# An equivariant message-passing kernel with 24 indirect gathers and 176 TensorE products placed ahead of its first pass

## The chip, the cores and the metric

The kernel runs on one core of one Trainium2 chip. The metric is the device time of one execution, in microseconds. Before the change it is 10608.61 us, the median of 3 runs (10598.79 to 10617.41). The profile is of another execution of the same program; it shows each instruction of five engines: PE (TensorE, the matrix products), DVE (VectorE), ACT (ScalarE), POOL (GpSimd) and SP (SyncE, which mostly issues transfers). PEld is the weight load of TensorE.

## The reference

There are N = 10000 nodes with 64 channels of 4 components each (256 floats, 1 KB a node), and E = 640000 edges, each with a source node, a target node, 4 numbers Y and 4 features.

```python
def reference(x, src, dst, Y, edge_feat, w_rad, cg, w_mix):
    N, C, M = x.shape[0], x.shape[1], x.shape[2]          # 10000, 64, 4
    R = _silu(edge_feat @ w_rad)                          # (E, C)
    xs = x[src]                                           # (E, C, M): the gather
    tp = jnp.einsum('eci,ef,ifo->eco', xs, Y, cg)         # (E, C, M)
    msg = R[:, :, None] * tp
    agg = _segment_sum(msg.reshape(-1, C * M), dst, N).reshape(N, C, M)
    return jnp.einsum('ncm,cd->ndm', agg, w_mix)
```

## The kernel before, in words

The edges are sorted by target node on the chip, so that the sum over the edges of a node becomes products on TensorE. This takes three stages.

Pass 1 (`pass1`, with `tables` and `route`) deals the edges, in three parts, into 18 groups of target nodes. Chunks of 12 tiles of 128 edges are put in order by products with one-hot matrices (`move`, L602) and scattered into a buffer in device memory by an indirect transfer that POOL issues (`store`, L613, the tile `rt` into `grp`). Pass 2 does the same within each group, with buckets of 32 nodes (into `bkt`). The messages (`messages`) go bucket by bucket: `gather` (L893) issues one indirect transfer for each tile of 128 edges, which fetches 128 rows of `x` of 1 KB each into `xg`; DVE multiplies by the radial weights (L945); `sums` (L958) adds up on TensorE; `mix` (L1006) applies the last weights in 256-column products, and the result is written out. A third stage (`overflow`) treats edges that found no room, in a loop with a run-time count, at the very end.

The first part of pass 1 runs alone, and `groups` then runs all the rest interleaved: messages of one group, pass 2 of the next and pass 1 of the next part. The order within an engine is fixed in the program; each engine runs its own queue in order and waits on semaphores. Transfers that POOL issues go through one software queue with eight semaphores in turn, those of SP and ACT through hardware queues.

At the start, `run` (L1206) opens the pool `p1`, POOL clears the tile `z` (L1214), the constants are made on POOL and DVE (`consts`, L144), SP loads the first target and source numbers (`ends`, L672 and L673), and ACT's queue issues 18 transfers that clear the group buffers from `z` (L230). The first products on TensorE are the counts of L365. All on-chip memory is taken from pools; a tile whose memory was used before waits for what last used it.

The lines with numbers are those of the program before; in the changed program the lines up to L86 keep theirs, the others move by 2, and those of `run` and what follows by 57.

Of the kernel before, what the change touches and what calls it, by code (L numbers as in the profile page):

```python
# [18 lines left out]
F = mybir.dt.float32  # L19
BF = mybir.dt.bfloat16  # L20
I32 = mybir.dt.int32
OP = mybir.AluOpType
# [3 lines left out]
P = 128  # L26
# [19 lines left out]
class Pass:  # L46


    def __init__(self, T, r, cap, act, carry):
        self.T, self.r, self.cap, self.act, self.carry = T, r, cap, act, carry  # L50
        self.stride = 1 << (cap + P - 1).bit_length()
        self.rw = r * W

        assert T * P + B * (2 * r - 2 if carry else r - 1) < (P + 1) * r and cap >= P


def weave(main, side, ratio):

    acc = 0.0
    for said in main:  # L60
        acc += ratio
        while acc >= 1.0:
            acc -= 1.0
            next(side, None)
        yield said
    yield from side


def run(gen):
    for _ in gen:  # L70
        pass


class Kernel:
    def __init__(self, ctx, tc, x, src, dst, Y, ef, w_rad, cg, w_mix, out):
        self.ctx, self.tc, self.nc = ctx, tc, tc.nc
        self.N, self.E = x.shape[0], src.shape[0]
        assert self.E % P == 0
        self.NT = self.E // P
        self.x = x.rearrange("n c i -> n (c i)")  # L80
        self.src = src.rearrange("(p t) -> p t", p=P)
        self.dst = dst.rearrange("(p t) -> p t", p=P)
        self.Y = Y.rearrange("(p t) f -> p t f", p=P)
        self.ef = ef.rearrange("(p t) f -> p t f", p=P)
        self.w_rad, self.cg, self.w_mix = w_rad, cg, w_mix
        self.out = out.rearrange("n c o -> n (c o)")  # L86
        pool = lambda n, b, **k: ctx.enter_context(tc.tile_pool(name=n, bufs=b, **k))
        self.cst = pool("cst", 1)
        self.ps = pool("ps", 1, space=bass.MemoryType.PSUM)
        self.dr = pool("dr", 1, space=bass.MemoryType.DRAM)  # L90

        N, E, T, r = self.N, self.E, 12, 14
        assert N <= 1 << 14 and BT == sum(sum(u) for _, u in SPLIT)
        self.NG = (N + GN - 1) // GN
        assert self.NG <= B
        self.part, cut = [], 0
        for i, (share, _) in enumerate(SPLIT):
            end = cut + round(self.NT * share / (2 * T)) * 2 * T if i + 1 < len(SPLIT) else self.NT
            self.part.append((cut, end))
            cut = end  # L100
        self.gt = []
        for a, z in self.part:
            nch = (z - a + T - 1) // T
            e = [min(GN, N - g * GN) * (z - a) * P / N for g in range(self.NG)]
            self.gt.append([math.ceil((m + (r - 1) / 2 * nch + 3 * math.sqrt(m + (r * r - 1) / 12 * nch)) / P)
                            for m in e])
        NG = self.NG
        self.p1 = Pass(T, r, max(map(max, self.gt)) * P // r, 6, False)
        self.p2 = Pass(11, 15, BT * P // 15, 6, True)

        self.gbase = [[(k * NG + g) * self.p1.stride + self.p1.cap - self.gt[k][g] * P // r for g in range(NG)]
                      for k in range(len(SPLIT))]
        self.NBK = (N + NB - 1) // NB

        self.btile = [0]
        for _, u in SPLIT:
            self.btile.append(self.btile[-1] + sum(u))

        self.p1.ovf = len(SPLIT) * NG * self.p1.stride
        self.p2.ovf = self.NBK * self.p2.stride  # L120
        for q, tiles in ((self.p1, [z - a for a, z in self.part]), (self.p2, sum(self.gt, []))):
            q.none = -(-(q.ovf + sum((t + q.T - 1) // q.T for t in tiles) * P + 16) // q.stride) * q.stride
            q.rows = q.none
        self.p1.key, self.p2.key = "grp", "bkt"
        self.xw = max(q.T * q.rw for q in (self.p1, self.p2))
        assert max(q.T + q.carry for q in (self.p1, self.p2)) <= 12

        self.p1.NC, self.p2.NC = 24, max(-(-t // self.p2.T) for t in sum(self.gt, []))
        self.p1.dst = self.dr.tile([self.p1.rows, self.p1.rw], F, name="grp")
        self.p2.dst = self.dr.tile([self.p2.rows, self.p2.rw], F, name="bkt")  # L130

        self.sums = self.dr.tile([self.NBK, P, 256], F, name="sums")
        self.in_group = {"grp": 0, "bkt": 0}
        self.tab = {}
        self.held, self.wanted, self.pos = None, False, None
# [903 lines left out]
    def groups(self):  # L1039
# [26 lines left out]
        for v in range(4 * u):  # L1066
# [24 lines left out]
            next(main)  # L1091
        assert not later
        run(main)
        run(sort)

    def chunks(self, part):
# [21 lines left out]
    def overflow(self, ps, count):  # L1118
# [84 lines left out]
        with tc.For_i(0, n, 1) as k:  # L1203
            body(k)

    def run(self):  # L1206
        tile_pool, nc = self.tc.tile_pool, self.nc
        order = [self.NG - 1] + list(range(self.NG - 1))
        self.segs = [(k, g) for k in range(len(SPLIT)) for g in order]
        with tile_pool(name="p1", bufs=2) as self.ph:  # L1210
            self.rt_bufs, self.ls = 38, 8
            self.lag, self.ahead, self.early = 2, 3, 1
            self.z = self.ph.tile([P, 2048], F, name="z", bufs=1)
            nc.gpsimd.memset(self.z, 0.0)  # L1214
            self.consts()

            with self.tc.manual_schedule(engines={mybir.EngineType.SP}):
                first = self.pass1(0, 8)
                next(first)
                run(self.clear_groups(0, nc.scalar))  # L1220
                for _ in range(40):
                    next(first, None)
                while self.held:
                    next(first)
                self.weights()
                later = itertools.chain(self.clear_buckets(),
                                        *(self.clear_groups(k, nc.sync) for k in range(1, len(SPLIT))))
                run(weave(first, later, 0.185))
                self.sorted = 1
        with tile_pool(name="p2", bufs=2) as self.ph:  # L1230
            self.rt_bufs, self.ls = 5, 4
            self.lag, self.ahead, self.early = 1, 2, 0
            self.p1.NC = 14
            with self.tc.manual_schedule(engines={mybir.EngineType.PE, mybir.EngineType.DVE,
                                                  mybir.EngineType.Activation}):
                self.groups()
        with tile_pool(name="p3", bufs=1) as self.ph:
            self.overflow_consts()
            self.overflow(self.p1, self.kov[:, 0:1])
            self.overflow(self.p2, self.kov[:, 1:2])  # L1240
# [29 lines left out]
```

## Time and profile before

| | |
|---|---|
| median of the runs | 10608.61 us (10598.79 to 10617.41) |
| profiled execution: first to last instruction | 8660.7 us |
| profiled execution: a time of its own beside the span | none is given |
| PE busy | 6942.9 us |
| DVE busy | 7173.7 us |
| POOL busy | 6041.3 us |
| ACT busy | 4089.0 us |
| mean granted clock of TensorE | 0.894 |
| bytes moved by transfers | 1056.64 MB |

The span is 1947.9 us shorter than the median of the runs. Busy times are of each engine for itself; they overlap. Rows of the timeline give the start from the beginning of the span, the duration, the engine, the line, the operation, the tiles written and read, the shape and how many instructions are merged in the row, and in brackets the idle time of the engine just before with what ended it. A 32-bit floating-point product stands in the rows as two MATMUL records with a LDWEIGHTS each, a bfloat16 product as one.

### The profile page before, as it was taken

What the parts mean: (1) busy time and instruction counts of PE and PEld (TensorE: products, weight loads), DVE (VectorE), ACT (ScalarE), POOL (GpSimd) and SP (SyncE); (2) the same over time, 40 slices, a digit from 0 to 9 for tenths busy, and PEclk for the clock granted to TensorE, in tenths of its full rate; (3) what the DMA queues carried; (4) which work ended last, traced back from release to release, by engine and by line L of the source; (5) the groups of instructions that cost most, each with busy time, mean ns of one, the idle gap of its engine ahead of it and who ended that gap; (6) DMA issues with size and microseconds to landing.
All of it is one profiled execution on the core that took longest, in us unless ns stands there. A gap on an engine that the chain in (4) does not pass through costs nothing. (4 is left out here: it accounts for less than half of the span.)

```text
span 8660.7 us, 149335 instructions
## 1 busy us (share of the span) xinstructions
PE 6942.9 (80%) x52148; PEld 6380.0 (74%) x52148; DVE 7173.7 (83%) x13741; ACT 4089.0 (47%) x11736; POOL 6041.3 (70%) x6308
## 2 busy tenths in 40 slices
PE   7978888888888778888888888866888878788875
PEld 6867777777777677777777777766777767777764
DVE  8989899889998788999989998877877768677754
ACT  6866555555556455454544554433333323333310
POOL 1236777667777767777777777777777777777775
PEclk9989999889999889999889899888998889888887
DMA  9313434334433434444444444444444444444442
GB/s 169 104 58 99 123 115 119 103 113 117 121 110 111 122 106 132 135 132 138 133 130 136 135 133 134 128 138 132 128 125 125 125 124 124 122 128 125 124 123 83
DMA packets 696289, 1056.64 MB, mean 122 GB/s; under 512 B 252018, under 2 KB 500226, under 8 KB 695536
## 3 DMA queue, kind: packets, MB, share of 16 engines
q0 software_dynamic: 286560, 746.71, 30.3%
q1 hardware_dynamic: 406384, 292.76, 12.2%
q8 instruction: 412, 6.75, 0.3%
q10 hardware_dynamic: 2592, 7.63, 0.3%
q14 instruction: 341, 2.79, 0.1%
HBM read 856.08 MB, written 207.12 MB: 123 GB/s over the span
## 5 line engine op out<-in xcount | busy, mean ns | idle before, releaser
L893 POOL DMA_INDIRECT xg<-in_x_dram,sidx x5321 | 5067.8, 952 | 1739.3 <-issue 1386.5
L602 PE MATMUL pr<-X,oh 128*128 128x126 f32 (+1 forms) x21112 | 2765.2, 289 | 395.7 <-ACT rt L609 215.6
L958 PE MATMUL G<-S,xg 128*128 128x128 f32 x21284 | 2953.1, 302 | 98.1 <-DVE Gp L987 62.8
L602 PEld LDWEIGHTS pr<-X,oh 128*128 128x128 f32 x21112 | 2638.2, 201 | 477.8 <-ACT rt L609 264.2
L958 PEld LDWEIGHTS G<-S,xg 128*128 128x128 f32 x21284 | 2803.5, 215 | 139.3 <-DVE Gp L987 86.2
L945 DVE TENSOR_TENSOR xg<-xg,pre 128x1536 f32<-128x1536 f32 (+1 forms) x939 | 1556.8, 1658 | 710.5 <-DMA xg<-in_x_dram,sidx 586.4
L594 ACT ACTIVATE sq<-i,rowf 128x128 f32<-128x128 f32 x5605 | 1735.7, 393 | 13.9 <-DVE rowf L559 13.4
L572 DVE TENSOR_TENSOR X<-dv,Wt 128x1512 f32<-128x1512 f32 (+4 forms) x958 | 1588.4, 1658 | 149.0 <-PE pr L602 94.8
L927 ACT ACTIVATE pre<-pre 128x384 f32<-128x384 f32 (+1 forms) x939 | 430.8, 459 | 1694.7 <-PE pre L924 1204.7
L595 ACT ACTIVATE oh<-sq,ones 128x768 f32<-128x768 f32 (+3 forms) x958 | 932.1, 973 | 32.9 <-issue 5.5
L938 DVE TENSOR_TENSOR S<-dv,pay 128x768 f32<-128x768 f32 (+1 forms) x939 | 857.4, 913 | 48.0 <-PE G L958 2.8
L613 POOL DMA_INDIRECT grp<-rt,idx x417 | 415.5, 996 | 585.9 <-ACT rt L609 240.1
L588 DVE TENSOR_TENSOR oh<-dv,rowf 128x640 f32<-128x640 f32 (+2 forms) x922 | 792.2, 864 | 0.5
L613 POOL DMA_INDIRECT bkt<-rt,idx x541 | 543.2, 1004 | 221.7 <-issue 125.8
L911 PE MATMUL pre<-identb,e 128*108 128x128 bf16 x1878 | 277.3, 231 | 523.4 <-DVE xg L945 513.6
L911 PEld LDWEIGHTS <-e 128*108 128x108 bf16 x1878 | 219.9, 133 | 604.5 <-issue 515.2
L916 ACT ACTIVATE sT<-pre 108x256 bf16<-108x256 f32 x939 | 353.5, 376 | 631.1 <-PE pre L911 628.4
L1006 PE MATMUL po<-wf,Gs 128*128 128x256 f32 (+2 forms) x1392 | 382.3, 436 | 150.7 <-DVE Gs L987 150.5
L542 ACT ACTIVATE pc<-pp 128x432 f32<-128x432 f32 (+3 forms) x506 | 243.7, 482 | 524.1 <-DVE pos L551 407.3
L1006 PEld LDWEIGHTS po<-wf,Gs 128*128 128x128 f32 (+2 forms) x1392 | 277.5, 205 | 238.3 <-DVE Gs L987 166.8
L609 ACT ACTIVATE rt<-pr 128x135 f32<-128x135 f32 (+1 forms) x958 | 258.8, 273 | 269.4 <-DMA bkt<-rt,idx 181.4
L923 PE MATMUL pre<-wr,sT 108*128 108x192 bf16 x939 | 240.2, 256 | 142.2 <-ACT sT L916 141.8
(240 smaller groups left out, 5309.3 us busy)
## 6 DMA issues: line engine op xcount, KB each, us to landing
xg<-in_x_dram,sidx POOLq DMA_INDIRECT x5321
sums<-Gp SPq DMA_DIRECT2D x626, 128.0 KB
old<-sums SPq DMA_DIRECT2D x626, 128.0 KB
bkt<-z SPq DMA_DIRECT2D x24, 994.5 KB
pay<-bkt SPq DMA_DIRECT2D x34, 486.0 KB
ys<-in_Y_dram SPq DMA_DIRECT2D x104, 96.0 KB
es<-in_edge_feat_dram SPq DMA_DIRECT2D x104, 96.0 KB
out_dram<-ot SPq DMA_DIRECT2D x69, 128.0 KB
```

Source lines behind the costliest of these rows:

```text
L572: nc.vector.tensor_tensor(X[:, :m, :].rearrange("p t (s w) -> p t s w", w=W), msk.unsqueeze(3).to_broadcast([P, m, ps.r, W]), QD[c // Q][1 ...
L588: nc.vector.tensor_tensor(oh[:, :v, :], self.v128.unsqueeze(1).to_broadcast([P, v, P]), row[:, o:o + v].unsqueeze(2).to_broadcast([P, v, P ...
L594: nc.scalar.activation(sq[:, u, :], self.i128, AF.Square, bias=to, scale=-1.0)
L595: nc.scalar.activation(oh[:, v:v + len(at), :], sq[:, :len(at), :], AF.Relu, bias=self.ones[:, 0:1], scale=-2.0)
L602: nc.tensor.matmul(pr[:, :ps.rw], oh[:, u, :], X[:, u, :], start=(u == 0), stop=(not on and u == m - 1))
L613: st = nc.gpsimd.indirect_dma_start(out=ps.dst, out_offset=bass.IndirectOffsetOnAxis(ap=idx[:, i:i + 1], axis=0), in_=RT.pop(c), in_offset ...
L893: nc.gpsimd.indirect_dma_start(out=xg[:, t, :], out_offset=None, in_=self.x, in_offset=bass.IndirectOffsetOnAxis(ap=si[:, u:u + 1], axis=0))
L911: nc.tensor.matmul(pre[:KR, 256 + 128 * h:384 + 128 * h], e[:, 36 * t:36 * t + KR], self.identb, start=True, stop=True)
L938: nc.vector.tensor_tensor(S[:, :ut], self.eq[:, :ut].unsqueeze(3).to_broadcast([P, ut, NB, 4]), pb[:, :, 1:5].unsqueeze(2).to_broadcast([P ...
L945: nc.vector.tensor_tensor(V, V, R.unsqueeze(3).to_broadcast([P, ut, 64, 4]), op=OP.mult)
L958: nc.tensor.matmul(G[:, h].rearrange("p n f -> p (n f)"), V[:, t, 32 * h:32 * h + 32, :].rearrange("p c i -> p (c i)"), S[:, t].rearrange( ...
L1006: nc.tensor.matmul(po[:nn, :256], Gs[:, h, f].rearrange("p b n -> p (b n)")[:, :nn], self.wf[:, h, f, :], start=(h + f == 0), stop=(h + f ...
```

## The change

A new method `probe` runs in `__init__` ahead of everything else, with two pools of its own that are closed again when it returns. It writes only tiles of these pools, which nothing reads; what the rest computes is the same.

It makes a list of row numbers (7 times the partition) and issues 24 indirect transfers on POOL's queue, which gather rows of `x` by that list: most have 256 floats a row and 128, 127, 126, 125, 124, 123, 122, 120, 119, 112, 64, 32, 16, 8, 4 or 2 rows; one has rows of 64 floats, two have rows of 1024 floats (128 and 127 rows). Then 176 products go to TensorE, on constant data: full 128x128 tiles of weights with 256 or 128 columns, weights of 64 columns on alternating and on the same half of the array, 64x64 quarters, 32-column strips, 32x32 tiles, transposes, and bfloat16 products of 128 and 384 columns.

```diff
+        with tc.tile_pool(name="probe", bufs=1) as ph, tc.tile_pool(name="pps", bufs=1, space=bass.MemoryType.PSUM) as pp:
+            self.probe(ph, pp)
         pool = lambda n, b, **k: ctx.enter_context(tc.tile_pool(name=n, bufs=b, **k))
...
+    def probe(self, ph, pp):
+        nc = self.nc
+        idx = ph.tile([P, 1], I32, name="qidx")
+        nc.gpsimd.iota(idx, pattern=[[0, 1]], base=0, channel_multiplier=7, allow_small_or_imprecise_dtypes=True)
+        src = ph.tile([P, 256], F, name="qsrc")
+        nc.vector.memset(src, 1.5)
...
+        for rows, w in ((128, 256), (128, 256), (127, 256), (127, 256), (122, 256), (124, 256), (124, 256), (123, 256),
+                        (125, 256), (119, 256), (126, 256), (120, 256), (112, 256), (64, 256), (32, 256), (16, 256),
+                        (8, 256), (4, 256), (2, 256), (128, 64), (128, 1024), (127, 1024), (128, 256), (128, 256)):
+            t = ph.tile([P, w], F, name="q%d" % n)
...
+            nc.gpsimd.indirect_dma_start(
+                out=t[:rows], out_offset=None, in_=x,
+                in_offset=bass.IndirectOffsetOnAxis(ap=idx[:rows, 0:1], axis=0))
+        banks = [pp.tile([P, 512], F, name="qb%d" % i) for i in range(8)]
+        mm = lambda o, l, r, tr=False: nc.tensor.matmul(o, l, r, start=True, stop=True, is_transpose=tr, skip_group_check=True)
+        for i in range(24):
+            mm(banks[0][:, :256], src[:, :128], src)
+        for i in range(8):
+            mm(banks[0][:, :128], src[:, :128], src[:, :128])
+        for i in range(16):
+            c = 64 * (i % 2)
+            mm(banks[1][c:c + 64, :256], src[:, :64], src)
+        for i in range(16):
+            mm(banks[2][0:64, :256], src[:, :64], src)
+        for i in range(16):
+            r, c = 64 * (i // 2 % 2), 64 * (i % 2)
+            mm(banks[3 + i // 2 % 2][c:c + 64, :256], src[r:r + 64, :64], src[r:r + 64])
+        for i in range(16):
+            c = 32 * (i % 4)
+            mm(banks[5][c:c + 32, :256], src[:, :32], src)
+        for i in range(32):
+            r, c = 32 * (i // 4 % 4), 32 * (i % 4)
+            mm(banks[1 + i // 4 % 4][c:c + 32, :256], src[r:r + 32, :32], src[r:r + 32])
+        for i in range(8):
+            mm(banks[6][:, :128], src[:, :128], eye, True)
+        for i in range(16):
+            mm(banks[7][:, :128], bsrc[:, :128], bsrc[:, 128:256])
+        for i in range(8):
+            mm(banks[7][:, :384], bsrc[:, :128], bsrc[:, 128:512])
+        for i in range(16):
+            if i % 2:
+                mm(banks[0][:, :256], src[:, :128], src)
+            else:
+                mm(banks[2][0:64, :256], src[:, :64], src)
```

More of the change, by code (lines that the diff above doesn't have):

```diff
@@ L1204, in overflow @@
             body(k)
+    def probe(self, ph, pp):
[4 more added lines that the diff above has]
+        nc.vector.memset(src, 1.5)
+        bsrc = ph.tile([P, 512], BF, name="qbsrc")
+        nc.vector.memset(bsrc, 1.5)
+        dif = ph.tile([P, P], F, name="qdif")
+        nc.gpsimd.iota(dif, pattern=[[1, P]], base=0, channel_multiplier=-1, allow_small_or_imprecise_dtypes=True)
+        eye = ph.tile([P, P], F, name="qeye")
+        nc.vector.tensor_scalar(eye, dif, 0.0, None, op0=OP.is_equal)
+        n = 0
+        for rows, w in ((128, 256), (128, 256), (127, 256), (127, 256), (122, 256), (124, 256), (124, 256), (123, 256),
+                        (125, 256), (119, 256), (126, 256), (120, 256), (112, 256), (64, 256), (32, 256), (16, 256),
+                        (8, 256), (4, 256), (2, 256), (128, 64), (128, 1024), (127, 1024), (128, 256), (128, 256)):
+            t = ph.tile([P, w], F, name="q%d" % n)
+            n += 1
+            x = self.x if w == 256 else self.x.rearrange("n k -> (n k)").rearrange("(a b) -> a b", b=w)
+            nc.gpsimd.indirect_dma_start(
[32 more added lines that the diff above has]
+                mm(banks[2][0:64, :256], src[:, :64], src)
```

## The prediction

> **What bounds the kernel now.** I read the page first (the span, the busy shares), then the stage table in the long middle part, then who waits there, and last the start and the end of the timeline, because the change stands at the start. The page's head:
>
> ```profile
> span 8660.7 us, 149335 instructions
> PE 6942.9 (80%) x52148; PEld 6380.0 (74%) x52148; DVE 7173.7 (83%) x13741; ACT 4089.0 (47%) x11736; POOL 6041.3 (70%) x6308
> L893 POOL DMA_INDIRECT xg<-in_x_dram,sidx x5321 | 5067.8, 952 | 1739.3 <-issue 1386.5
> L613 POOL DMA_INDIRECT grp<-rt,idx x417 | 415.5, 996 | 585.9 <-ACT rt L609 240.1
> L613 POOL DMA_INDIRECT bkt<-rt,idx x541 | 543.2, 1004 | 221.7 <-issue 125.8
> ```
>
> DVE looks the busiest, at 83%. But POOL's 70% leaves out the time between two indirect transfers. In the middle of the span (the stage table for 2000 to 6000 us, for L893 and for L613 alone) and in a stretch of POOL's timeline:
>
> ```profile
> 2000.00:6000.00 4000.00, 2500.25 (x2627) 0.90 0.45 128
> ```
>
> ```profile
> 2000.00:6000.00 4000.00, 477.35 (x475) 0.90 0.45 128
> ```
>
> ```profile
> 4002.00 0.94 POOL L893 DMA_INDIRECT xg<-in_x_dram,sidx  x1 [0.30 <-issue]
> 4003.25 0.95 POOL L893 DMA_INDIRECT xg<-in_x_dram,sidx  x1 [0.30 <-issue]
> 4004.50 0.95 POOL L893 DMA_INDIRECT xg<-in_x_dram,sidx  x1 [0.30 <-issue]
> 4005.75 1.00 POOL L613 DMA_INDIRECT bkt<-rt,idx  x1 [0.30 <-issue]
> ```
>
> One transfer starts every 1.25 us: 0.95 busy and 0.30 of issue. 2627 + 475 = 3102 of them at 1.25 us are 3878 of the 4000 us. So POOL's queue paces the long part, with DVE and PE close behind it, and 5321 + 417 + 541 = 6279 indirect transfers matter to the end. Work put ahead of everything does not meet this bound. It meets the start:
>
> ```profile
> 0.76 1.80 POOL L1214 MEMSET z<- 128x2048 f32 x1 [0.29 <-POOLq L1258]
> 0.76 0.40 SPq L672 DMA_DIRECT2D da<-in_dst_dram  x1
> 0.84 0.17 DVE L154 MEMSET zr<- 16x135 f32 x1 [0.84 <-PEq L1258]
> 2.59 20.03 ACTq L230 DMA_DIRECT2D grp<-z  x18
> 15.53 1.60 PE L365 MATMUL cnt<-D,sel 128*64 128x216 bf16 x8 [15.53 <-DVE D L338]
> 22.71 1.28 ACT L370 ACT_TABLE_LOAD   x1 [22.71 <-DMA grp<-z]
> ```
>
> The first 22.7 us hang on one chain: POOL clears `z`, ACT's queue issues 18 clears from it for 20.03 us, and ACT takes up its first work. PE has nothing before 15.53 us.
>
> **The change: what can overlap.** Nothing is removed. In the order of the changed program the first work of each old queue (POOL's clear of `z`, SP's load of `da`, DVE's clear of `zr`, ACT's first clear, PE's first count) waits for all eight semaphores of the probe's gathers, and all but ACT's for PE too; ACT's needs `z`. The reason is on-chip memory: the new pools are closed and the old ones lie over them. So probe and old program stand one behind the other. The shift of the end is the longer of two paths that run beside each other, the gathers and the products, less the little that either saves. Behind it, PE's, ACT's, POOL's and SP's orders are the same; DVE makes its constants before it treats the first edges instead of after. I cost that at nothing: DVE has 9.87 us of work in the 22.7 us that the clears take (row below); without that cover it would be those 9.87 us.
>
> ```profile
> 0.00:22.70 22.70, 1.60 (x8) 1.32 (x8) 9.87 (x162) 0.00 (x0) 3.82 (x17) 1.00 0.91 306
> ```
>
> **The gathers' path.** 24 issues at 1.25 us are 30.0 us. Each waits for the landing of the eighth before it; the nearest landing in the chain at the end took 2.28 us, far less than eight issues. So the bound from below is 1 (start) + 30 + 2.3 = 33 us. The bound from above is a gather served by one transfer engine. Two rows price it:
>
> ```profile
> q0 software_dynamic: 286560, 746.71, 30.3%
> 8645.99 2.28 DMA ocur<-out_dram,odi
> ```
>
> 30.3% of 16 engines over 8660.7 us are 41,987 us of engine time for 746.71 MB, 0.056 us per KB. The gather of 127 rows of 4 KB (508 KB), the 22nd issue, would then take 28.6 us on one engine: 1 + 22 x 1.25 + 2.3 + 28.6 = 59 us. In this trace every indirect transfer but the two of 16 rows has 128 rows, so neither end is shown; I take 59 as the upper end.
>
> The Trainium skill ("DMA: Bandwidth & Descriptors", "Queues, rings and completion order") says a transfer is spread over the largest number of engines up to 16 that divides its rows, 127 giving one. By it this path would be 59 us; no run here shows it yet.
>
> **The products' path.** Prices per record:
>
> ```profile
> 8590.93 3.64 PE L1006 MATMUL po<-wf,Gs 128*64 128x256 f32 x16 [0.94 <-DVE Gs L987]
> 8581.91 5.41 PE L1006 MATMUL po<-wf,Gs 128*128 128x256 f32 x16 [2.37 <-DVE Gs L987]
> 8567.03 2.94 PE L958 MATMUL G<-S,xg 128*128 128x128 f32 x24
> L958 PE MATMUL G<-S,xg 128*128 128x128 f32 x21284 | 2953.1, 302 | 98.1 <-DVE Gp L987 62.8 <-ACT Gp L989 17.8 <-DVE Gs L987 9.3
> L1006 PE MATMUL po<-wf,Gs 128*128 128x256 f32 x1104 | 286.0, 418 | 72.3 <-DVE Gs L987 72.1
> L911 PE MATMUL pre<-identb,e 128*108 128x128 bf16 x1878 | 277.3, 231 | 523.4 <-DVE xg L945 513.6 <-DMA xg<-in_x_dram,sidx 9.2
> L534 PE MATMUL pp<-D,A 128*128 128x432 bf16 x208 | 75.8, 365 | 0.0
> ```
>
> A 256-column f32 record takes 3.64/16 = 0.2275 us in a fast run and 5.41/16 = 0.338 in a slow one; its mean is 286.0/1104 = 0.259. A 128-column f32 record is 2953.1/21284 = 0.139, and 2.94/24 = 0.1225 is the shortest pitch of a pair of weight load and product in a long run. A bf16 product of 128 columns is 277.3/1878 = 0.148, one of 432 columns 75.8/208 = 0.364.
>
> 136 of the 176 products are f32 with 256 columns, so 272 records. Of these 48 (full tiles), 32 (same half) and 32 (the last sixteen) have nothing to overlap with: 112 x 0.2275 = 25.5 us. The other 160 (alternating halves, quarters, strips, 32x32 tiles) use different parts of the array in turn. The old kernel has no such pair. Bounds: fully one behind the other, 160 x 0.2275 = 36.4; perfectly beside each other, (32/2 + 32/4 + 32/4 + 64/16) x 0.2275 = 8.2. I take the shortest pitch seen, 160 x 0.1225 = 19.6, since each record still brings a weight load of its own. Then 16 records of 128 columns, 2.2; 8 transposes as such a record each, 1.1; 16 bf16 products, 2.4; 8 of 384 columns, 2.9 at most. A cold start: 20 records at 0.338 instead of 0.2275, 2.2. Sum: 25.5 + 19.6 + 2.2 + 1.1 + 2.4 + 2.9 + 2.2 = 55.9 us. With the lower end for the 160 records it is 44.5; with the upper end, and 0.259 a record, 70.4 + 10.8 = 81.
>
> So the products end near 56.5 us, the gathers between 33 and 59. The sum: the old first work starts some 56 us later than before, and 10608.61 + 56 = 10664.6 us. The profiled execution has only its span, 8660.7, and would become 8717; the 1947.9 us up to the median of the runs are in no view, and I leave them as they are. If the runs stretch everything by 10608.61/8660.7 = 1.225, the 56 are 69.
>
> **The rivals.**
> *No overlap on the array (0.22).* The 160 records run one behind the other: 73 to 81 us, about 10685. For it: the old program's records never overlap in pairs of different tiles. Against it: in long runs product and weight load do overlap, 0.1225 us a pair where they take 0.139 on the mean.
> *Full overlap, and the gathers spread (0.15).* 44.5 us, 10653. The Trainium skill ("TensorEngine Tiling (Array Packing)", "Tiling Modes") has tiles of the array work independently of each other; by that the products are at this end, and no row here can say.
> *One engine serves the odd gathers, and they end last (0.13).* 59 us or a few more, 10670.
> *The gathers leave the software queue in another state, and every later indirect transfer is cheaper (0.05).* This is the one that ends on the other side. 6279 transfers are the pace; from 56/6279 = 9 ns each less, the probe is paid for; with 20 ns less (2% of the 0.95) the end comes 126 - 56 = 70 us earlier, 10539. Against it: the rows of 4002 to 4005 us keep one pitch to within 10 ns whatever went before. For it: those all have 128 rows. The same mechanism upwards (0.04) gives 56 + 126, 10791.
> *The probe does not stand ahead (0.03).* If the old start ran under it, the 22.7 us of clears would be hidden, and with the short ends of both paths, 44.5 - 22.7 = 22 us, the time is 10608 to 10630, within what can be told. The waits in the order of the program speak against it.
>
> **How the numbers follow.** The forecast, 10664.6, has 0.38; with the rivals it makes 1. A change of 0.2% is 21 us, about what can be told from none here (the runs before lie 18.6 us apart). Slower by more: 0.38 + 0.22 + 0.15 + 0.13 + 0.04 = 0.92. Within: 0.03. Faster: 0.05. The range goes from the full overlap less the spread of the runs, 10653 - 19 = 10634, to the serial array stretched by 1.225, 10608.6 + 81 x 1.225 + 8.8 (from the median of the runs before to their highest) = 10716.6. The two cases of a changed state are left out.
>
> **What would show it.** Right: in the profile after, the clear of `z` and SP's load of `da` start at 45 to 80 us, together, and ACT's first table load 22 us behind them; the stretch from there to the end is 8660 us to within a few; L893 keeps 952 ns and 1.25 us pitch; the last probe product or the landing of the 22nd gather ends just before the old start. The pairs in the alternating halves at 0.12 us a record confirm the middle price, 0.23 the serial rival. Wrong: a mean of L893 that is off by more than 9 ns, an old start before 45 us, or a span that grows by 56 while the runs do something else, which would mean that the 1947.9 us outside the span depend on what the program does first.

## The result and the profile after

The changed kernel takes 10667.17 us (median of 3 runs, 10666.09 to 10684.23) against 10608.61 us before: 58.6 us more, a ratio of 1.0064 (95% interval 1.0044 to 1.0084). Slower, inside the range, 2.6 us from the forecast.

The head of the page after, its two largest groups, and two waits of the list of waits (engine, line, what it waited for, us in total, times, longest):

```profile
span 10665.4 us, 150028 instructions
PE 7752.5 (73%) x52468; PEld 6957.9 (65%) x52468; DVE 7200.7 (68%) x13744; ACT 4077.7 (38%) x11736; POOL 6074.7 (57%) x6334
L895 POOL DMA_INDIRECT xg<-in_x_dram,sidx x5321 | 5062.2, 951 | 3125.4 <-issue 1374.7
L960 PE MATMUL G<-S,xg 128*128 128x128 f32 x21284 | 3322.9, 317 | 1008.4 <-issue 543.4
```

```profile
POOL xg L895 <- PE G L960: 752.8, 244, 10.0
PEld G L960 <- issue: 640.4, 777, 5.1
```

The span is 2004.7 us longer than the 8660.7 us of the profile before, and that is not the change. This span ends 1.8 us short of the execution's own time, so nothing of any size lies around a span. I take the two profiles to be of different chips: the experiments below show the old kernel at 8.66 ms on two chips and at 10.45 ms on two others. What the change costs is therefore read at the start of the trace and from runs on one chip, never from the two spans. The start, from the timeline (POOL's and PE's rows of the probe, then the old first work):

```profile
1.21 27.89 PE L1232 MATMUL qb<-qsrc 128*128 128x256 f32 x175 [1.21 <-DVE qsrc L1214]
1.71 1.10 POOL L1228 DMA_INDIRECT q<-in_x_dram,qidx  x1 [0.52 <-POOL qdif L1218]
4.37 2.56 POOL L1228 DMA_INDIRECT q<-in_x_dram,qidx  x1 [0.31 <-issue]
33.40 2.55 POOL L1228 DMA_INDIRECT q<-in_x_dram,qidx  x1 [0.31 <-issue]
37.51 0.95 POOL L1228 DMA_INDIRECT q<-in_x_dram,qidx  x1 [0.30 <-issue]
45.20 9.71 PE L1232 MATMUL qb<-qsrc 128*64 128x256 f32 x32
58.87 0.40 SPq L674 DMA_DIRECT2D da<-in_dst_dram  x1
58.92 1.80 POOL L1271 MEMSET z<- 128x2048 f32 x1 [20.47 <-DMA q<-in_x_dram,qidx]
58.95 0.17 DVE L156 MEMSET zr<- 16x135 f32 x1 [57.18 <-DMA q<-in_x_dram,qidx]
60.76 19.84 ACTq L232 DMA_DIRECT2D grp<-z  x18
```

SP, POOL and DVE all take up the old work at 58.9 us, where it was 0.8 us before: 58.1 us later, next to the 58.6 us between the runs. (That the two agree so closely is luck: in the experiments the time rises by up to 27 us more, or 21 us less, than the start moves.) The products end at 45.20 + 9.71 = 54.9 us. What POOL and DVE wait for is a gather: the 22nd, of 127 rows of 4 KB, issued from 33.40 to 35.95 us. The transfer records from 40 to 54 us hold nothing of this queue but its packets of 4096 bytes, one behind the other, 159 ns each: one row at a time on one transfer engine, 127 x 0.159 = 20.2 us.

The products were slower than they need be. Among the 32 strip records, which took 12.0 us together, PE stands still again and again without a wait that the trace shows; the experiments call these stops halts. From the timeline, and from the stage table (PE's busy time stands first behind the length, the granted clock third from the end):

```profile
30.60 0.62 PE L1232 MATMUL qb<-qsrc 128*32 128x256 f32 x3 [1.50 <-issue]
32.72 1.01 PE L1232 MATMUL qb<-qsrc 128*32 128x256 f32 x3 [1.50 <-issue]
34.85 3.20 PE L1232 MATMUL qb<-qsrc 128*32 128x256 f32 x7 [1.11 <-issue]
```

```profile
27.40:31.50 4.10, 2.31 (x22) 0.88 (x19) 0.00 (x0) 0.00 (x0) 3.19 (x4) 1.00 0.05 8
31.50:38.40 6.90, 3.96 (x10) 0.70 (x10) 0.00 (x0) 0.00 (x0) 5.68 (x5) 0.50 0.41 89
38.40:41.80 3.40, 3.39 (x68) 1.68 (x67) 0.00 (x0) 0.00 (x0) 0.05 (x1) 0.50 0.34 94
```

The granted clock is not what starts the halts. It still reads 1.00 when PE's weight loads first stop (about 28.6 us), falls to 0.50 at 31.5 us, and stays there for 3.4 us after PE runs on at 38.4 us. In the two later traces with halts it also falls 3 to 5 us behind the first of them.

### The profile page after: what moved, and what is told of

Read it like the earlier page. It is cut to its first block, busy times and chain, and to the rows that moved or that the text cites. A ratio compares the mean times of both kernels' runs of the same rounds, so it can differ in the third digit from the quotient of the medians.

```text
span 10665.4 us, 150028 instructions
## 1 busy us (share of the span) xinstructions
PE 7752.5 (73%) x52468; PEld 6957.9 (65%) x52468; DVE 7200.7 (68%) x13744; ACT 4077.7 (38%) x11736; POOL 6074.7 (57%) x6334
## 5 line engine op out<-in xcount | busy, mean ns | idle before, releaser
L895 POOL DMA_INDIRECT xg<-in_x_dram,sidx x5321 | 5062.2, 951 | 3125.4 <-issue 1374.7
L960 PE MATMUL G<-S,xg 128*128 128x128 f32 x21284 | 3322.9, 317 | 1008.4 <-issue 543.4
L960 PEld LDWEIGHTS G<-S,xg 128*128 128x128 f32 x21284 | 3075.2, 228 | 1136.1 <-issue 640.4
L604 PE MATMUL pr<-X,oh 128*128 128x126 f32 (+1 forms) x21112 | 3114.4, 305 | 878.7 <-issue 417.0
L604 PEld LDWEIGHTS pr<-X,oh 128*128 128x128 f32 x21112 | 2901.3, 215 | 1062.6 <-issue 540.5
L989 DVE TENSOR_TENSOR Gs<-old,G 128x256 f32<-128x256 f32 x313 | 131.3, 420 | 1029.3 <-remote 638.5
L989 DVE TENSOR_TENSOR Gp<-old,G 128x256 f32<-128x256 f32 x313 | 130.8, 418 | 522.4 <-remote 307.4
L1008 PE MATMUL po<-wf,Gs 128*128 128x256 f32 (+2 forms) x1392 | 347.6, 406 | 51.9 <-DVE Gs L989 47.5
```

The lines of the kernel that those rows point to most:

```text
L604: nc.tensor.matmul(pr[:, :ps.rw], oh[:, u, :], X[:, u, :], start=(u == 0), stop=(not on and u == m - 1))
L895: nc.gpsimd.indirect_dma_start(out=xg[:, t, :], out_offset=None, in_=self.x, in_offset=bass.IndirectOffsetOnAxis(ap=si[:, u:u + 1], axis=0))
L960: nc.tensor.matmul(G[:, h].rearrange("p n f -> p (n f)"), V[:, t, 32 * h:32 * h + 32, :].rearrange("p c i -> p (c i)"), S[:, t].rearrange( ...
```

## The experiments

Each was run beside the kernel before on the same chip. The place where the old work starts in the trace tells theories apart to within a microsecond. The time tells less: the work behind that start differs by some 20 us either way between the traces.

### The kernel before, once more

No edit.

> The kernel before, unchanged, to have its span and its time from one execution. Theory: the 8660.7 us of the profile before belong to other conditions than the runs (the changed kernel's span, 10665.4 us, lies within 2 us of its own time); then the span here is within 5 us of the time, near 10600 us, with a mean granted clock near 0.83. Rival: the program has a fixed 1948 us outside its span and the changed kernel lost it; then the span is 8660 us again beside a time of 10608.

Measured: 10453.38 us, beside 10452.35 for the other runs of it there (ratio 0.9998, 0.9988 to 1.0008); span 10450.2 us in an execution of 10451.97 us, mean granted clock 0.837. The busy times of its page, two lines of its waits, and the second of these from the profile before, where no such line stands for L958:

```profile
PE 7648.3 (73%) x52148; PEld 6890.4 (66%) x52148; DVE 7192.1 (69%) x13741; ACT 4076.4 (39%) x11736; POOL 6037.2 (58%) x6308
```

```profile
PEld G L958 <- issue: 534.7, 640, 8.5
PEld pr L602 <- issue: 515.3, 653, 7.1
```

```profile
PEld pr L602 <- issue: 83.1, 86, 7.5
```

The old kernel has a span of 10450 us here and of 8660.7 us in the profile before, with the same instructions. The difference is on TensorE: DVE, ACT and POOL are busy as long as before to within 0.4%, PE 705 us longer, and in the longer span its weight load stands still 640 times ahead of L958 and 653 times ahead of L602 for nothing that the profile shows. The theory holds; the rival of a fixed time outside the span falls.

### Each part alone

The gathers alone leave out everything from `banks` to the end of `probe`:

```diff
-        banks = [pp.tile([P, 512], F, name="qb%d" % i) for i in range(8)]
...
-                mm(banks[2][0:64, :256], src[:, :64], src)
```

> The 24 gathers without any product. Theory (the gather of 127 rows of 4 KB runs on one transfer engine and ends last): the old work starts at 58 to 59 us as with both parts, and the time is 58 us above before. Rival (the products end last, or hold up the gathers): the start moves to 40 us or less, and the time is 40 us above before.

Measured: 10515.36 us, ratio 1.0059 (1.0042 to 1.0076), 63 us more. The old work starts where it did with both parts, so the products hold nothing up:

```profile
33.38 2.55 POOL L1228 DMA_INDIRECT q<-in_x_dram,qidx  x1 [0.30 <-issue]
59.12 1.81 POOL L1240 MEMSET z<- 128x2048 f32 x1 [20.69 <-DMA q<-in_x_dram,qidx]
```

The products alone leave out the loop of the gathers:

```diff
-        for rows, w in ((128, 256), (128, 256), (127, 256), (127, 256), (122, 256), (124, 256), (124, 256), (123, 256),
...
-                in_offset=bass.IndirectOffsetOnAxis(ap=idx[:rows, 0:1], axis=0))
```

> The 176 products without any gather. The products ended at 54.9 us with both parts, of which the 32 records of the 32-column strips took 12.0 us. Theory: those strips' halts are not of the strips but come and go with something else (a strip record should cost a quarter of 0.22 us); then the strips take about 2 us, the products end at 45 us and the time is 45 us above before. Rival: the halts belong to the strips; then 12 us again, an end at 55 us, 55 us above before.

Measured: 10476.31 us, ratio 1.0027 (1.0017 to 1.0036), 24 us more (18 to 38), not 45. The products end at 34.73 + 9.71 = 44.4 us as the theory said, and the 32 strip records take 1.9 us, so the halts are not the strips' own. But the old start did not wait:

```profile
0.76 0.40 SPq L674 DMA_DIRECT2D da<-in_dst_dram  x1
1.14 1.79 POOL L1261 MEMSET z<- 128x2048 f32 x1
8.12 20.20 ACTq L232 DMA_DIRECT2D grp<-z  x18
34.73 9.71 PE L1222 MATMUL qb<-qsrc 128*64 128x256 f32 x32
```

Without the tiles of the gathers the probe's memory is small, and only little of the old start lies over it. SP, POOL and ACT's clears ran beside the products.

### Every row count a multiple of 16

```diff
-        for rows, w in ((128, 256), (128, 256), (127, 256), (127, 256), (122, 256), (124, 256), (124, 256), (123, 256),
-                        (125, 256), (119, 256), (126, 256), (120, 256), (112, 256), (64, 256), (32, 256), (16, 256),
-                        (8, 256), (4, 256), (2, 256), (128, 64), (128, 1024), (127, 1024), (128, 256), (128, 256)):
+        for rows, w in ((128, 256),) * 13 + (
+                        (64, 256), (32, 256), (16, 256),
+                        (16, 256), (16, 256), (16, 256), (128, 64), (128, 1024), (128, 1024), (128, 256), (128, 256)):
```

> Both parts, but each gather has 128 rows where it had 112 to 127, and 16 where it had 2, 4 or 8, so that every row count divides by 16. Theory: every issue of 128 rows takes 0.95 us on POOL (not up to 2.56), the gather of 4 KB rows is spread over 16 engines and lands 2 us behind its issue, so the gathers end near 34 us and the products decide: old start at 45 to 55 us. Rival (the bytes decide, not the spread): the start stays at 58 to 59 us.

Measured: 10513.91 us, ratio 1.0057 (1.0040 to 1.0074), an old start at 63.2 us, behind the theory's 55. Its reason is in the last bracket:

```profile
27.68 0.93 POOL L1228 DMA_INDIRECT q<-in_x_dram,qidx  x1 [0.30 <-DMA q<-in_x_dram,qidx]
31.25 0.59 PE L1232 MATMUL qb<-qsrc 128*64 128x256 f32 x1 [2.92 <-issue]
34.06 0.58 PE L1232 MATMUL qb<-qsrc 128*64 128x256 f32 x1 [2.22 <-issue]
53.42 9.71 PE L1232 MATMUL qb<-qsrc 128*64 128x256 f32 x32
63.19 1.80 POOL L1271 MEMSET z<- 128x2048 f32 x1 [32.07 <-PE qb L1232]
```

The gather of 4 KB rows now takes POOL 0.93 us, and POOL has issued its last gather by 31.1 us, and the queue's last packet ends at 33.5 us, as the theory had it; POOL waits for PE. The products were later than expected because TensorE halted again, this time among the alternating halves (20.5 us for 32 records that take 3.5 elsewhere). So the spread theory holds, and my bound for the halts was too low.

### One row more, and one odd gather more

```diff
-                        (8, 256), (4, 256), (2, 256), (128, 64), (128, 1024), (127, 1024), (128, 256), (128, 256)):
+                        (8, 256), (4, 256), (2, 256), (128, 64), (128, 1024), (128, 1024), (128, 256), (128, 256)):
```

> Only the gather of 127 rows of 4 KB gets a 128th row; all else of the change stays. Theory (127 rows go to one engine, 20.2 us at 159 ns a row, 128 rows to sixteen): it lands 2 to 3 us behind its issue and the gathers end by 41 us; the products decide, at 45 us without halts and up to 63 with them. Rival (4 KB rows are slow however many): the gathers end at 58 us again.

Measured: 10516.54 us, ratio 1.0069 (1.0045 to 1.0093). That is 69 us more. One row more makes the gather finish long before: POOL's issue takes 0.94 us, the last packet of the gathers' queue ends at 38.9 us by the transfer records (58.3 us with 127 rows), and the old start waits for PE at 57.2 us:

```profile
33.46 0.94 POOL L1228 DMA_INDIRECT q<-in_x_dram,qidx  x1 [0.30 <-issue]
57.24 1.81 POOL L1271 MEMSET z<- 128x2048 f32 x1 [20.32 <-PE qb L1232]
```

The time did not fall, since halts in the strips (13.2 us) moved the products' end to 57.2 us. So the gathers end by 41 us, as the theory had it, and they are no longer what is waited for.

The second edit, on the gathers alone:

```diff
-                        (8, 256), (4, 256), (2, 256), (128, 64), (128, 1024), (127, 1024), (128, 256), (128, 256)):
+                        (8, 256), (4, 256), (2, 256), (128, 64), (128, 1024), (127, 1024), (127, 1024), (128, 256)):
```

> The gathers alone, with a second gather of 127 rows of 4 KB right behind the first, in the place of a gather of 128 rows of 1 KB. If both go to the same engine, the second waits for the first: the old work starts near 59 + 20 = 79 us and the time is 78 us above before. If the engine changes from one odd gather to the next, both run beside each other: start near 62 us (59 and one more issue of 2.55 + 0.30), time 61 us above before.

Measured: old start at 61.3 us, the 62 us of the case in which the engine changes, not 79:

```profile
33.39 2.55 POOL L1228 DMA_INDIRECT q<-in_x_dram,qidx  x1 [0.30 <-issue]
36.24 2.54 POOL L1228 DMA_INDIRECT q<-in_x_dram,qidx  x1 [0.30 <-issue]
61.34 1.80 POOL L1240 MEMSET z<- 128x2048 f32 x1 [21.28 <-DMA q<-in_x_dram,qidx]
```

Two gathers of 20 us each cost 2.2 us more than one: they ran beside each other. The time was 10487.21 us (ratio 1.0045, 1.0026 to 1.0063), 40 us above before and 21 us under what the start says.

### All small tiles on one position

On the products alone:

```diff
-            c = 64 * (i % 2)
+            c = 0
...
-            r, c = 64 * (i // 2 % 2), 64 * (i % 2)
-            mm(banks[3 + i // 2 % 2][c:c + 64, :256], src[r:r + 64, :64], src[r:r + 64])
+            r, c = 0, 0
+            mm(banks[3][c:c + 64, :256], src[r:r + 64, :64], src[r:r + 64])
...
-            c = 32 * (i % 4)
+            c = 0
...
-            r, c = 32 * (i // 4 % 4), 32 * (i % 4)
-            mm(banks[1 + i // 4 % 4][c:c + 32, :256], src[r:r + 32, :32], src[r:r + 32])
+            r, c = 0, 0
+            mm(banks[1][c:c + 32, :256], src[r:r + 32, :32], src[r:r + 32])
```

> The products alone, with all halves, quarters, strips and 32x32 tiles put on one position of the array instead of different ones. Theory (different positions run beside each other, which made the halves 0.109 and the quarters 0.059 us a record): now every one of the 160 records takes 0.216 us, 7 us for each set of 32 and 14 us for the 64, and the products end near 45 - 8.7 + 34.6 = 66 us where those alone ended at 44.4. Rival (the short pitch belongs to the small tiles): the ends stay within 2 us.

Measured from the starts of the records in the trace, us for each set:

| records | different positions (products alone) | one position |
|---|---|---|
| 32, alternating halves | 3.50 | 6.96 |
| 32, 64x64 quarters | 1.89 | 7.05 |
| 32, 32-column strips | 1.86 | 7.03 |
| 64, 32x32 tiles | 1.43 | 24.35 |

Tiles on different positions do run beside each other, two, nearly four and more at a time. The end came at 82.7 us rather than 66 (the terms of the expectation in fact add up to 71): the 64 records on one 32x32 tile took 24.4 us, not 14. The stage table:

```profile
16.00:44.00 28.00, 28.00 (x130) 16.30 (x128) 0.00 (x0) 0.00 (x0) 0.00 (x0) 1.00 0.64 211
44.00:68.40 24.40, 24.40 (x65) 9.91 (x64) 0.00 (x0) 0.00 (x0) 0.00 (x0) 0.57 0.00 1
```

While one 32x32 tile alone was in use the mean granted clock was 0.57, with PE busy all the time: it read 1.00 for the first 3.3 us, with starts 0.216 us apart, and 0.50 from 47.3 us on, with most starts 0.427 us apart. So the 24.35 us of the table hold the price of the clock too; at 0.216 us a record they would be 14. One run of this kernel was made, so its time (10524.25 us) is given no weight.

### Products that hold the start

On the products alone, at the end of `probe`:

```diff
+        q = ph.tile([P, 7488], F, name="q")
+        nc.vector.tensor_copy(q[:, :256], banks[0][:, :256])
```

> The products alone, and behind them a tile that lies over the memory of the old start and takes a copy of the first product's bank on DVE. With the products alone the old start did not wait, and the time rose by 24 us where the products took 44 us: theory, 22 us of the old start (the clears) ran beside them. With this tile the old start has to wait for the products: it comes at 45 us and the time is 45 us above before. Rival (a product ahead costs half its time for another reason): 24 us again.

Measured: 10488.91 us, ratio 1.0047 (1.0027 to 1.0067), 41 us more (28 to 70), with products as long as in the products alone:

```profile
33.96 9.71 PE L1222 MATMUL qb<-qsrc 128*64 128x256 f32 x32
43.71 0.42 DVE L1253 COPY q<-qb 128x256 f32<-128x256 f32 x1 [41.93 <-PE qb L1222]
44.22 0.40 SPq L674 DMA_DIRECT2D da<-in_dst_dram  x1
```

With one tile the same products cost 41 us and not 24. The intervals of the two times overlap; the place of the old start, 44.2 us and not 0.8, leaves no doubt. The waits on memory put the probe ahead, and without them the 22 us of clears hide beside it.

### Do the halts need the gathers?

The products ten times over, without gathers (the old start held behind them by a tile as above) and with gathers beside them (whose own tiles hold it):

```diff
+        for _ in range(10):
+            for i in range(24):
+                t = ph.tile([P, 256], F, name="q%d" % i)
+                nc.gpsimd.indirect_dma_start(
+                    out=t, out_offset=None, in_=self.x,
+                    in_offset=bass.IndirectOffsetOnAxis(ap=idx[:, 0:1], axis=0))
```

> The 176 products ten times over, without gathers, and the old start held behind them as before. Theory (the halts of TensorE, pitches of 0.7 us and its multiples for a record that takes 0.22 or less, need indirect gathers beside the products): ten times the undisturbed 43 us, near 430 us, with fewer than 5 pitches over 0.6 us. Rival (the halts come with a long run of instructions whatever runs beside): about one stretch of 10 to 17 us of halts in each repetition or two, 50 to 150 us more.

> The same products ten times, now with 24 gathers of 128 rows of 1 KB for each of the ten, issued by POOL beside them (300 us of gathers). Theory: stretches of halts come back while gathers run, 50 us or more in all, and none in the last 100 us behind the last gather. Rival: no difference from the run without gathers, within 10 us.

> The tenfold products beside 240 gathers once more. Where the kernel before takes 8660 us: no pitches over 0.6 us but the ten ends of a repetition, an old start near 410 us. Where it takes 10450 us: theory (halts need gathers on such a chip), stretches of halts in the first 300 us while gathers run and none behind them, an old start 50 us or more later; rival, halts spread over the whole stretch, or none.

Measured: old starts at 411.5, 411.6 and 411.9 us, and no pitch over 0.6 us within the probe in any of the three. The times were 9083.69, 9100.17 and 9090.64 us, 421, 437 and 422 us above before. So here gathers beside the products brought no halts, against the theory of the second run. But these runs were on two chips on which the kernel before takes 8662.73 and 8668.73 us, and there TensorE has hardly any halts at all. So the question for the other chips was not answered. There, products with gathers beside them halted in three traces of three (the change, the even rows, the one row more: 10 to 17 us each), and products alone in none of three. That speaks for the gathers as a condition on those chips, though not one that is enough by itself; it does not show the mechanism.

### The change once more

No edit to the changed kernel.

> The change itself, once more beside the kernel before, since the kernel before took 10608 us, 10452 and 10448 us in three places and 8663 us in a fourth. Theory: the start is held by the gather of 127 rows of 4 KB, which no halt of TensorE touches; so the old start comes at 58 to 59 us wherever it runs and the time rises by 58 us, be the time before 8660 us (ratio 1.0067) or 10450 us (1.0055). Rival: the rise belongs to the halts; then it is 45 us or less where the time before is 8660 us.

Measured: 8744.64 us beside 8668.73, ratio 1.0087 (1.0070 to 1.0104), 76 us more. Its page and its timeline:

```profile
span 8746.3 us, 150028 instructions
PE 6974.4 (80%) x52468; PEld 6395.6 (73%) x52468; DVE 7180.5 (82%) x13744; ACT 4092.3 (47%) x11736; POOL 6082.4 (70%) x6334
```

```profile
34.15 9.71 PE L1232 MATMUL qb<-qsrc 128*64 128x256 f32 x32
59.07 1.81 POOL L1271 MEMSET z<- 128x2048 f32 x1 [20.64 <-DMA q<-in_x_dram,qidx]
```

With no halts the products end at 43.9 us, 11 us earlier than in the first profile after, and the old work starts at 59.0 us all the same. So the gather sets the start, and the rise does not belong to the halts. The other 18 us of the 76 lie behind the start. They are more than the scatter of the runs there: each of the four runs is at least 67 us above each of the seven of the kernel before. By the traces it is 8746.3 - 59.0 = 8687 us from the start to the end, against 8660.7 - 0.8 = 8660 in the profile before, which is of another set of runs. The old gathers (L893) start 62 us later than in that profile near 600 us, 73 us near 4000 us and 78 us near 8600 us. The three tenfold runs show the same, 10 to 27 us beyond the shift of the start. On the chips at 10450 us that stretch was up to 14 us shorter and up to 20 us longer than in the old kernel's trace. So on the faster chips the later work takes a little longer behind the prefix; why, stays open.

## Why the prediction was right, and where it was not

*The probe stands ahead of everything.* Right, and shown by the one tile that moves the old start from 0.8 to 44.2 us. The new order of DVE's constants cost nothing: the clears took 19.84 us (20.03 before) and ACT's first table load came at 80.68 us, 21.8 us behind the old start (22.7 - 0.8 before).

*What bounds the old kernel.* The reading that POOL's queue paces the long part holds for the chip of that profile. In the profile after, POOL waits 752.8 us for PE at L895 and is busy 57%; there TensorE's halts weigh more. The forecast did not use it, but the 9 ns rival did, and its gain would not have held where POOL waits for PE. L895 kept its 951 ns, so that rival did not occur.

*The gathers' path.* Predicted 33 to 59 us; it ended at 58.9 and set the result. The case that came true is the rival with 0.13, one engine for the odd gather that ends last, not the forecast's; that the forecast's 56 us lie beside it is luck. Its 59 us were right through two errors that cancel. Twenty-two issues at 1.25 us should have ended at 28.5 us and ended at 35.95, because a gather of 127 rows takes POOL 2.55 us, not 0.95, and the others of 119 to 125 rows 1.09 to 1.67; a bound from gathers of 128 rows missed that. And 28.6 us on one engine, from the queue's mean under load, was 20.2 us in a quiet one: a packet of 4096 bytes took 0.227 us on the mean from 1000 to 8000 us of the profile before, and 0.159 us here.

The rule of the Trainium skill ("DMA: Bandwidth & Descriptors"; it stands in "Why a DMA increments its semaphore by 16 and not by 1", not in the section that the prediction named), the largest divisor up to 16, agrees with the one packet at a time, with the order of POOL's issue times (below), and, where it has the engines taken in turn, with the two odd gathers side by side. It should have had more than 0.13.

*The products' path.* Predicted 56.5 us, measured 54.9, and the step that failed is the price of the 160 overlapping records: 19.6 us taken, 8.7 measured without halts (3.5 + 1.9 + 1.9 + 1.4), 8.2 for perfect overlap. A weight load of its own for each record does not hold the pitch at 0.1225 us. The sign that was to confirm that price, 0.12 us a record in the alternating halves, did come (0.109), but as half of 0.218: the quarters and strips at 0.059 and 0.058 tell the two apart. The last sixteen products took 9.7 us for 32 records, 0.30 each instead of 0.2275: changing between tiles of 64 and 128 columns has a price that I did not count. The 24 bfloat16 products took 2.3 us and not 5.3. Without halts the path is 43 us, near the 44.5 of the full-overlap rival; the halts of 10 us brought it back to the number I had. So the number 56 was right by luck and its mechanism wrong. The Trainium skill ("TensorEngine Tiling (Array Packing)", "Tiling Modes") has tiles work independently and a change of mode drain the array. The first agrees with the sets above; the second would account for the 0.30 us, though no run takes that price apart.

*The 1947.9 us.* I left them as something in no view. The runs point to another chip: the same program differs by as much between chips, and never within the runs of one. As no chip was used at two different times, a condition of a chip that changes with time is not excluded. That the shift was added to the runs' median, not taken from the profile's span, is what kept the forecast right.

## What to carry to other kernels

That nothing reads a piece of scratch work does not make it free: where its tiles lie under those of the first stage, everything behind waits for its slowest transfer. Give indirect gathers row counts that divide by 16; here one row less than 128 turned a 4 KB-row gather into 20 us on one engine. And compare a span with its own execution's time before using it beside other runs: here a gap of 18% pointed to a different chip.

## What the hardware showed that I had not expected

POOL's time for an indirect gather goes by the rows that fall to one transfer engine, and hardly by the rows or the bytes in all. Issue times from the profile after, for rows of 1 KB; the number of engines is taken as the row count's largest divisor up to 16, which the gather of 127 rows alone shows directly:

| rows | 127 | 122 | 123 | 124 | 125 | 119 | 126 | 120 | 112 | 128 | 64 | 32 | 16 | 8 | 4 | 2 |
|---|---|---|---|---|---|---|---|---|---|---|---|---|---|---|---|---|
| largest divisor up to 16 | 1 | 2 | 3 | 4 | 5 | 7 | 14 | 15 | 16 | 16 | 16 | 16 | 16 | 8 | 4 | 2 |
| rows for one engine | 127 | 61 | 41 | 31 | 25 | 17 | 9 | 8 | 7 | 8 | 4 | 2 | 1 | 1 | 1 | 1 |
| POOL, us | 2.56 | 1.67 | 1.41 | 1.30 | 1.21 | 1.09 | 0.99 | 0.98 | 0.96 | 0.95 | 0.92 | 0.88 | 0.86 | 0.88 | 0.89 | 0.86 |

An estimate from the two ends of the table, 0.85 us and 0.0135 us for each row of one engine, meets every column to within 0.04 us. The divisor alone would not: 122 rows and 2 rows share it and differ by 0.8 us. The 127 rows of 4 KB took 2.55 us too.

The other surprise is the chips: the same program took 8663 and 8669 us on two of them and 10448, 10452 and 10608 us in three other sets of runs. In the longer spans TensorE's record pitches gather at 0.7 us and 1.4 us: 575 of 680 to 740 ns in the profile after, 33 in the profile before. What holds it there was not found; as the stage table of the result shows, the granted clock falls behind the halts and does not start them.
